# Starting a fused attention and MLP kernel with the v products of two x tiles, and spreading two chunks' row factors by a product

## The chip, the cores and the metric

The kernel runs on one core of one Trainium2 chip. Its engines are TensorE (PE, matrix products), VectorE (DVE), ScalarE (ACT), GpSimd (POOL) and SyncE (SP, which here issues nearly all DMAs); each works through its own queue of instructions in program order. The metric is the time of one execution in microseconds (us), as the median over several runs.

## The reference

The input x has 2048 rows of 512 numbers in bf16. The core of the reference, shortened:

```python
xn = layernorm(x)                       # no scale, no shift, eps 1e-5
q, k, v = split(xn @ wqkv)              # 32 heads of 16; row s attends to rows s, s-2, ..., s-14
s = softmax(q @ k_window * 0.25) @ v_window @ wo
h = gelu(layernorm(xn) @ w1)            # the norm is taken a second time
hs = shift_rows_by_group(h) @ w2        # four column groups, moved by +1, -1, +2, -2 rows
x1 = xn + hs
y = x1 + gelu(layernorm(x1) @ w3) @ w4  # w3: 512 x 1376, w4: 1376 x 512
out = x + s * silu(y)
```

The second norm acts on rows that are normed already, so it only multiplies each row by a factor close to 1, 1/sqrt(r² var + eps), where var is the variance of the row of x and r = 1/sqrt(var + eps). This text calls these the row factors.

## The kernel before

Rows are split by parity (even rows p = 0, odd rows p = 1), so that a window with a step of two becomes a plain window. Each half has two chunks of 512 rows, so there are chunks 0 to 3, and each chunk has four tiles of 128 rows. PSUM has eight banks: six are handed out as three pairs in turn (`pair`), two singly in turn (`single`, banks 6 and 7). Every instruction keeps its place in the program (`pin`), so the order of the calls in the text is the order on each engine's queue.

The first part of the kernel, up to about 50 us, is what the change touches. For each chunk it does this:

- `load_x` brings x tiles in. The loads stand first in SP's queue: four single tiles of chunk 0, then the q columns of wqkv, its v columns, its k columns (512 KB each), then chunk 1, w1 and chunk 2.
- `Norm.stats` (L217) takes mean and variance on DVE (`bn_stats`, `bn_aggr`); `root_act` (L223) gets 1/sqrt by ACT's Sqrt and a DVE reciprocal (chunk 0 only), `root` (L228) by two POOL instructions; `apply` (L231) norms in place on DVE.
- `turn` (L277) transposes two normed tiles by eight 128-wide products with the identity into one single bank, and DVE copies them to `xnT`.
- `rows2` (L244) computes the row factors r2, as 128 partitions x 4 numbers: for chunk 0 on DVE and ACT, for the others on POOL. `rows2_spread` (L260) must lay them along the free dimension, the same on all partitions: a PE transpose to 4 x 128, a DVE copy, a DMA to DRAM, and a DMA back that repeats the row over the 128 partitions into the last quarter of the tile `xn2T`. `scaled` (L269) multiplies `xnT` by it on DVE, and `w1` (L370) takes the product with w1 and a gelu on ACT.
- `q_half`, `q_all`, `k_all`, `v_mm`, `v_pair` are the projections; ACT moves their results out of PSUM: q as it is (`q_keep`), k twice with a mask `em` per head parity into `kM` (L327), v into a staging tile `vst` that must hold zeros elsewhere (L346), from where SP's queue writes it to DRAM (L350).

Before any data is there, twelve 128x512 products of ones (L139) run on PE, DVE clears `vst`, `zero` and the edges of `kM` and sums the identity into `em`. Chunk 0 is started by halves of 256 columns: two tiles are normed and transposed together, the q product of that half is taken, then v of two tiles, then the second half. Lines 488 to 549 are the order written out by hand. After them come w2 (L388), w3 and w4, and the attention in 18 blocks with the w4 products laid between.

Of the kernel before, what the change touches and what calls it, by code (L numbers as in the profile page):

```python
# [9 lines left out]
ALU = mybir.AluOpType  # L10
# [10 lines left out]
def kernel(  # L21
# [19 lines left out]
    def pin(ins):  # L41

        return tc.keep_in_program_order(ins)
# [38 lines left out]
    def b8(shape, name):  # L82
        return big.tile(shape, BF16, name=name, tag="b8")

    def b4(shape, name):
        return sm4.tile(shape, BF16, name=name, tag="b4")
# [4 lines left out]
    def pair():  # L91
        cnt["d"] += 1
        b = 2 * ((cnt["d"] - 1) % 3)
        return PS[:, b : b + 2, :]
# [8 lines left out]
    def load_x(c, t0, n):  # L103
        p, i = c // 2, (c % 2) * TPC + t0
        pin(SP.dma_start(
            out=xn[p][:, i : i + n, :], in_=xv[p, i * P : (i + n) * P, :].rearrange("(i q) d -> q i d", q=P)
        ))

    for t in range(TPC):
        load_x(0, t, 1)  # L110
    wqk_sb = b8([P, ND, 2 * D], "wqk_sb")
    pin(SP.dma_start(out=wqk_sb[:, :, 0:D], in_=wqkv_v[:, :, 0:D]))
    wv_sb = b4([P, ND, D], "wv_sb")
    pin(SP.dma_start(out=wv_sb, in_=wqkv_v[:, :, 2 * D : 3 * D]))
    pin(SP.dma_start(out=wqk_sb[:, :, D : 2 * D], in_=wqkv_v[:, :, D : 2 * D]))
    load_x(1, 0, 2)
    load_x(1, 2, 2)
# [17 lines left out]
    eps_t = const.tile([P, 1], F32, name="eps_t")  # L135
    pin(DVE.memset(eps_t[:], EPS))

    for i in range(12):
        pin(PE.matmul(  # L139
            PS[:, 6 + i % 2, :], lhsT=ones_bf[:], rhs=ones_bf.unsqueeze(1).to_broadcast([P, TPC, P]),  # L140
            start=True, stop=True,
        ))
# [12 lines left out]
    def head_masks():  # L155
        pin(DVE.tensor_reduce(
            out=em, in_=ident.rearrange("p (g e d) -> p e g d", e=2, d=16), op=ALU.add, axis=mybir.AxisListType.XY
        ))
# [49 lines left out]
    class Norm:  # L208
# [11 lines left out]
            for j in range(lo, hi):  # L220
                pin(DVE.bn_aggr(out=self.mv[:, j, :], in_=self.st[:, j, :]))

        def root_act(self, lo, hi):  # L223
            r = self.rstd[:, lo:hi]
            pin(ACT.activation(r, self.mv[:, lo:hi, 1], AF.Sqrt, bias=eps_t[:]))
            pin(DVE.reciprocal(out=r, in_=r))

        def root(self):  # L228
            rsqrt_eps(self.rstd, self.mv[:, :, 1])
# [8 lines left out]
    def x_of(c):  # L238
        p, k = c // 2, c % 2
        return xn[p][:, k * TPC : (k + 1) * TPC, :]  # L240
# [3 lines left out]
    def rows2(c, ln):  # L244

        r2 = small_t("r2", [P, TPC])
        r2b = small_t("r2b", [P, TPC], BF16)
        eng = DVE if c == 0 else POOL
        pin(eng.tensor_tensor(out=r2, in0=ln.rstd, in1=ln.rstd, op=ALU.mult))
        pin(eng.tensor_tensor(out=r2, in0=r2, in1=ln.mv[:, :, 1], op=ALU.mult))  # L250
        if c == 0:
            pin(ACT.activation(r2, r2, AF.Sqrt, bias=eps_t[:]))
            with nc.allow_low_precision("bf16 row factors"):
                pin(DVE.reciprocal(out=r2b, in_=r2))
        else:
            rsqrt_eps(r2, r2)
            pin(POOL.tensor_copy(out=r2b, in_=r2))
        r2s[c] = r2b

    def rows2_spread(c):  # L260
        pt = single().bitcast(BF16)[0:TPC, 0:P]
        pin(PE.transpose(pt, r2s[c], ident[:]))
        t = small_t("r2t", [TPC, P], BF16)
        pin(DVE.tensor_copy(out=t, in_=pt))
        pin(SP.dma_start(out=r2_d[c].rearrange("(j q) -> j q", q=P), in_=t))
        xn2Ts[c] = b4([P, ND, CH], "xn2T")
        pin(SP.dma_start(out=xn2Ts[c][:, ND - 1, :], in_=r2_d[c : c + 1, :].to_broadcast([P, CH])))

    def scaled(c):  # L269
        p, k = c // 2, c % 2  # L270
        t = xn2Ts[c]
        pin(DVE.tensor_tensor(
            out=t, in0=xnT[p][:, :, k * CH : (k + 1) * CH],
            in1=t[:, ND - 1, :].unsqueeze(1).to_broadcast([P, ND, CH]), op=ALU.mult,
        ))

    def turn(c, h):  # L277
        p, k = c // 2, c % 2
        i = k * TPC + 2 * h
        pt = single().bitcast(BF16).rearrange("p (a j q) -> p a j q", a=ND, j=2)  # L280
        for j in range(2):
            for dt in range(ND):
                pin(PE.transpose(pt[:, dt, j, :], xn[p][:, i + j, dt * P : (dt + 1) * P], ident[:]))  # L283
        pin(DVE.tensor_copy(
            out=xnT[p][:, :, i * P : (i + 2) * P], in_=pt.rearrange("p a j q -> p a (j q)")
        ))

    def q_half(pts, lo, hi):
        for nt in range(ND):
            for dt in range(ND):  # L290
                pin(PE.matmul(  # L291
                    pts[nt // 2][:, nt % 2, lo:hi], lhsT=wqk_sb[:, dt, nt * P : (nt + 1) * P],
                    rhs=xnT[0][:, dt, lo:hi], start=(dt == 0), stop=(dt == ND - 1),
                ))
# [21 lines left out]
            q_keep(c, a, proj(c, a, wqk_sb[:, :, 0:D], chunk(xnT, c)))  # L316

    def k_pad(p):
        pin(DVE.memset(kM[p][:, :, 0:8, :], 0.0))
        pin(DVE.memset(kM[p][:, :, M + 8 : MK, :], 0.0))  # L320

    def k_all(c):
        p, k = c // 2, c % 2
        for a in range(2):
            pt = proj(c, a, wqk_sb[:, :, D : 2 * D], chunk(xnT, c))
            for e in range(2):
                pin(ACT.activation(  # L327
                    kM[p][:, 2 * a : 2 * a + 2, 8 + k * CH : 8 + (k + 1) * CH, e], pt, AF.Copy, scale=em[:, e : e + 1]
                ))
# [3 lines left out]
    def v_mm(p, t, pt):  # L333
        for dt in range(ND):
            pin(PE.matmul(  # L335
                pt, lhsT=xnT[p][:, dt, t * P : (t + 1) * P], rhs=wv_sb[:, dt, :],
                start=(dt == 0), stop=(dt == ND - 1),
            ))

    def v_keep(p, t, n, pt, later=None):  # L340
        st = vst[vn["n"] % 2]
        vn["n"] += 1
        src = ap_of(pt, [pt.ap[0], [16, 2], [32, 16 * n], [1, 16]])
        d = st[:, 0, 0, :]
        dst = ap_of(d, [d.ap[0], [2 * D + 16, 2], [32, 16 * n], [1, 16]])
        pin(ACT.activation(dst, src, AF.Copy))  # L346

        def put():
            for i in range(n):
                pin(SP.dma_start(  # L350
                    out=v_d[p][8 + (t + i) * P : 8 + (t + i + 1) * P], in_=st[:, :, i, :]
                ))

        if later is None:
            put()
        else:
            later.append(put)

    def v_pair(p, t):
        pt = pair()  # L360
        for i in range(2):
            v_mm(p, t + i, pt[:, i, :])
        v_keep(p, t, 2, pt[:, 0, :])

    def v_pad(p):
        rows = v_d[p].rearrange("r e d -> (r e) d")
        pin(SP.dma_start(out=rows[0:16], in_=zero[0:16, :]))
        pin(SP.dma_start(out=rows[2 * (M + 8) : 2 * MK], in_=zero[0:4, :]))

    def w1(c, a):  # L370
        p, k = c // 2, c % 2
        pt = proj(c, a, w1_sb, xn2Ts[c])
        pin(ACT.activation(  # L373
            hT[p][:, 2 * a : 2 * a + 2, 1 + k * CH : 1 + (k + 1) * CH], pt, AF.Gelu_apprx_tanh
        ))
# [86 lines left out]
    for p in range(2):  # L462
        pin(POOL.memset(hT[p][:, :, 0:1], 0.0))
        pin(POOL.memset(hT[p][:, :, M + 1 : M + 2], 0.0))
        pin(POOL.memset(qT[p][:, :, M:MQ], 0.0))
    pin(DVE.memset(vst[0], 0.0))
    pin(DVE.memset(vst[1], 0.0))
    pin(DVE.memset(zero, 0.0))
    k_pad(0)
    k_pad(1)  # L470
    head_masks()
    l0 = Norm(x_of(0), x_of(0), TPC, "l1")
    l0.stats(0, 2)
    l0.root_act(0, 2)
    l0.apply(0, 2)
    l0.stats(2, 3)
    turn(0, 0)
    l0.stats(3, 4)
    l0.root_act(2, 4)
    l0.apply(2, 4)  # L480
    rows2(0, l0)
    pin(ACT.preload_act_table_set("gelu_apprx_tanh_and_others"))
    pq = [pair(), pair()]
    q_half(pq, 0, 2 * P)
    pv = pair()
    v_mm(0, 0, pv[:, 0, :])
    turn(0, 1)
    v_mm(0, 1, pv[:, 1, :])
    rows2_spread(0)
    v_keep(0, 0, 2, pv[:, 0, :])  # L490
    load_x(3, 0, 2)
    load_x(3, 2, 2)
    l1 = Norm(x_of(1), x_of(1), TPC, "l1")
    l1.stats(0, 4)
    l1.root()
    q_half(pq, 2 * P, CH)
    for a in range(2):
        q_keep(0, a, pq[a])
    cnt["d"] -= 1
    scaled(0)  # L500
    l1.apply(0, 4)
    rows2(1, l1)
    pin(SP.dma_start(out=w2_sb, in_=B_w2.rearrange("(g q) n -> q g n", q=P)))
    k_all(0)
    v_pair(0, 2)
    v_pad(0)
    l2 = Norm(x_of(2), x_of(2), TPC, "l1")
    l2.stats(0, 2)
    w1(0, 0)
    rows2_spread(1)  # L510
    pin(SP.dma_start(out=w3_sb, in_=B_w3.rearrange("(dt q) f -> q dt f", q=P)))
    turn(1, 0)
    turn(1, 1)
    w1(0, 1)
    l2.stats(2, 4)
    l2.root()
    l2.apply(0, 4)
    rows2(2, l2)
# [3 lines left out]
    scaled(1)  # L522
    q_all(1)
    k_all(1)
    rows2_spread(2)
    v_pair(0, 4)
    l3.apply(0, 4)
    rows2(3, l3)
    v_pair(0, 6)
    w1(1, 0)  # L530
    turn(2, 0)
    turn(2, 1)
    rows2_spread(3)
    w1(1, 1)
    scaled(2)
    q_all(2)
# [5 lines left out]
        in_=B_w4[0 : (NF - 1) * P, :].rearrange("(ft q) n -> q ft n", q=P),  # L542
    ))
    pin(SP.dma_start(out=w4_sb[0:FL, NF - 1, :], in_=B_w4[(NF - 1) * P : F, :]))
    w1(2, 0)
    w1(2, 1)
    scaled(3)
    w1(3, 0)
    w1(3, 1)
    w2(0)  # L550
# [401 lines left out]
```

## Time and profile before

The median of three runs is 201.47 us (201.37 to 202.03). The profiled execution took 201.1 us; its span, from the first to the last instruction, is 199.3 us.

| engine | busy us | share of the span |
|---|---|---|
| PE, products | 189.3 | 95% |
| PE, weight loads (beside the products) | 92.0 | 46% |
| ACT | 128.5 | 64% |
| DVE | 117.9 | 59% |
| POOL | 19.4 | 10% |

Busy time of PE includes the tail of each product, of which the next one covers most: a 128x512 product is listed with 379 ns, but in a dense run one starts every 216 ns, a 128x256 one every 109 ns and a 128x128 one every 56 ns. So starts are compared here, not ends. In the timeline a line gives start, length, engine, source line, operation, operands, count, and in brackets the idle time before it and what ended that. "L301" is line 301 of the kernel before; for a helper it is the same for all of its callers.

### The profile page before, as it was taken

Reading aid. Unit: us, or ns where it says so; the run is one execution under the profiler, and the core shown is the slowest. Engines: PE = TensorE matmul, PEld = TensorE weight load, DVE = VectorE, ACT = ScalarE, POOL = GpSimd, SP = SyncE. Lnnn points to the kernel's source line nnn. Section 1 sums busy time; section 2 is a strip of 40 time slices with the busy share of each in tenths; the row PEclk is TensorE's granted clock in tenths of the full one; section 3 lists DMA queues with packets and bytes.
Section 4 is the critical chain, followed back from the end, with each engine's and each line's share of the span. In section 5 each row is a group of like instructions: output and inputs, shape, how many; then the busy total and the mean of one; then the engine's idle time right before and its main releaser. Section 6 shows DMA issues by size and latency. Waiting matters only on the chain.

```text
span 199.3 us, 5290 instructions
## 1 busy us (share of the span) xinstructions
PE 189.3 (95%) x2285; PEld 92.0 (46%) x2285; DVE 117.9 (59%) x234; ACT 128.5 (64%) x143; POOL 19.4 (10%) x52
## 2 busy tenths in 40 slices
PE   7799999999999999999999999999999999999990
PEld 2464544554444444444444444554445445454540
DVE  7876785522076697585100034654769878796694
ACT  2188759558817615345564788687878868877850
POOL 1008058000002022015000000000000000000000
PEclk9999999999999999999999999999999999999997
DMA  5977655654000433853650062565944655762433
GB/s 129 369 239 240 216 119 209 221 174 135 0 0 3 132 83 105 210 107 106 149 170 0 0 187 79 166 193 151 268 134 122 166 167 150 175 188 71 146 105 105
DMA packets 33878, 28.37 MB, mean 142 GB/s; under 512 B 10808, under 2 KB 32832, under 8 KB 33856
## 3 DMA queue, kind: packets, MB, share of 16 engines
q1 hardware_dynamic: 33568, 27.84, 47.0%
q8 instruction: 18, 0.29, 0.6%
q10 hardware_dynamic: 288, 0.20, 0.3%
q14 instruction: 4, 0.03, 0.0%
HBM read 17.27 MB, written 8.67 MB: 130 GB/s over the span
## 4 chain that ended last, share of the span: by engine, by line
PE 79%; DVE 10%; ACT 4%; DMA 4%; issue 1%; SPq 0%; ACTq 0%; DVEq 0%
PE PS L442 19%; PE PS L301 17%; PE PS L729 16%; PE PS L776 7%; PE PS L400 4%; PE PS L335 4%; DMA ring<-rec_d 3%; ACT kM L327 3%; PE PS L617 3%; PE PS L591 2%; PE PS L760 2%; PE PS L291 2%; PE PS L627 2%; PE PS L283 1%; DVE l3s L219 1%; DVE xn L408 1%
## 5 line engine op out<-in xcount | busy, mean ns | idle before, releaser
L442 PE MATMUL PS<-x1nT,w_sb 128*128 128x512 bf16 (+1 forms) x176 | 38.3, 379 | 0.1
L598 ACT ACTIVATE prob<-PS 128x1824 bf16<-128x1824 f32 x18 | 30.4, 1688 | 5.4 <-PE PS L591 4.7
L729 PE MATMUL PS<-w_sb,h3a 128*128 128x512 bf16 x128 | 32.7, 380 | 0.7 <-DVE xn L742 0.7
L448 ACT ACTIVATE h3a<-PS 128x1024 bf16<-128x1024 f32 x16 | 16.4, 1023 | 20.9 <-PE PS L442 20.9
L742 DVE TENSOR_TENSOR xn<-PS,xn 128x512 bf16<-128x512 f32 x15 | 10.2, 680 | 30.7 <-PE PS L729 30.5
L442 PEld LDWEIGHTS <-w_sb 128*128 128x128 bf16 (+1 forms) x176 | 17.5, 100 | 20.8 <-DMA x1nT<-x1n_dram 0.6
L301 PE MATMUL PS<-xnT,wqk_sb 128*128 128x512 bf16 x112 | 25.0, 379 | 0.0
L327 ACT ACTIVATE kM<-PS,em 128x1024 bf16<-128x1024 f32 x16 | 20.6, 1401 | 3.7 <-PE PS L301 3.7
L603 DVE TENSOR_TENSOR prob<-prob,maskb 128x1824 bf16<-128x1824 bf16 x18 | 19.8, 1102 | 3.6 <-ACT prob L598 3.6
L408 DVE TENSOR_TENSOR xn<-PS,xn 128x1024 bf16<-128x1024 f32 x8 | 9.6, 1213 | 14.7 <-PE PS L400 14.7
L729 PEld LDWEIGHTS <-h3a 128*128 128x128 bf16 x128 | 11.3, 97 | 14.1 <-issue 1.9
L301 PEld LDWEIGHTS <-wqk_sb 128*128 128x128 bf16 x112 | 10.9, 98 | 12.7
L776 PE MATMUL PS<-wo_sb,oT 128*128 128x512 bf16 (+1 forms) x68 | 15.5, 366 | 0.0
L301 PE MATMUL PS<-xn2T,w_sb 128*128 128x512 bf16 x64 | 14.8, 379 | 0.1
L400 PE MATMUL PS<-w_sb,hT 128*128 128x512 bf16 x64 | 14.5, 379 | 0.1
L729 PE MATMUL PS<-w_sb,h3b 128*128 128x512 bf16 (+1 forms) x48 | 13.5, 381 | 0.0
L312 ACT ACTIVATE qT<-PS 128x1024 bf16<-128x1024 f32 x8 | 8.1, 1023 | 7.8 <-PE PS L301 7.7
L786 ACT ACTIVATE sg<-PS 128x512 bf16<-128x512 f32 x14 | 8.3, 596 | 6.2 <-PE PS L776 6.1
L346 ACT ACTIVATE vst<-PS 128x512 bf16<-128x512 f32 (+1 forms) x12 | 8.8, 744 | 3.5 <-ACT sig L749 2.4
L373 ACT ACTIVATE hT<-PS 128x1024 bf16<-128x1024 f32 x8 | 8.1, 1035 | 4.5 <-PE PS L301 4.5
L219 DVE BATCH_NORM_STATS2 l3s<-xn 128x6 f32<-128x512 bf16 x16 | 10.2, 682 | 0.2
L219 DVE BATCH_NORM_STATS2 l1s<-xn 128x6 f32<-128x512 bf16 x16 | 10.1, 677 | 0.0
(98 smaller groups left out, 225.7 us busy)
## 6 DMA issues: line engine op xcount, KB each, us to landing
ring<-v_d SPq DMA_DIRECT2D x18, 256.0 KB
v_d<-vst SPq DMA_DIRECT2D x16, 256.0 KB, 2.9
x1n_dram<-xn SPq DMA_DIRECT2D x4, 512.0 KB
xo<-in_A_x_dram SPq DMA_DIRECT2D x8, 256.0 KB, 4.0
ring<-rec_d SPq DMA_DIRECT2D x4, 456.0 KB, 5.2
out_dram<-xo SPq DMA_DIRECT2D x7, 256.0 KB, 3.1
xn<-in_A_x_dram SPq DMA_DIRECT2D x6, 256.0 KB, 4.1
w_sb<-in_B_w_dram SPq DMA_DIRECT2D x1, 1376.0 KB, 7.5
```

The costliest lines, as they stand in the source:

```text
L219: pin(DVE.bn_stats(out=self.st[:, j, :], in_=self.src[:, j, :]))
L301: pin(PE.matmul(pt[:, b, :], lhsT=w[:, dt, nt * P : (nt + 1) * P], rhs=rhs[:, dt, :], start=(dt == 0), stop=(dt == ND - 1),))
L327: pin(ACT.activation(kM[p][:, 2 * a : 2 * a + 2, 8 + k * CH : 8 + (k + 1) * CH, e], pt, AF.Copy, scale=em[:, e : e + 1]))
L400: pin(PE.matmul(pt[:, j, :], lhsT=w2_src(p, g, m0), rhs=w2_sb[:, g, :], start=(g == 0), stop=(g == ND - 1),))
L408: pin(DVE.tensor_tensor(out=xs, in0=pts[h], in1=xs, op=ALU.add))
L442: pin(PE.matmul(pt[:fs, ft % 2, :], lhsT=w3_sb[:, dt, ft * P : ft * P + fs], rhs=x1nT[:, dt, :], start=(dt == 0), stop=(dt == ND - 1),))
L448: pin(ACT.activation(t[:, o : o + 2, :], pt, AF.Gelu_apprx_tanh))
L598: pin(ACT.activation(pr, S_ps[:, :, 0 : ND * NQ], AF.Exp, scale=SCALE))
L603: pin(DVE.tensor_tensor(out=f, in0=f, in1=maskb[:], op=ALU.min))
L729: pin(PE.matmul(pt, lhsT=h3_of(c, ft)[:fs, jj * P : (jj + 1) * P], rhs=w4_sb[:fs, ft, :], start=(ft == 0), stop=(ft == NF - 1 and silu < 2),))
L742: pin(DVE.tensor_tensor(out=x_i, in0=pt, in1=x_i, op=ALU.add))
L776: pin(PE.matmul(pt[:, 0:W], lhsT=oT[p][:, dt, i * P : (i + 1) * P], rhs=wo["sb"][:, dt, c], start=(dt == 0), stop=(dt == ND - 1),))
```

## The change

- Loads: after two x tiles the v columns come, then the other two x tiles, then the q columns. The issuing queue is the same.
- Ten products of ones instead of twelve.
- Filling with zeros moves: one `vst` tile to ACT (a Copy with scale 0 of 128x2048), `zero` and the edges of `kM` to POOL, one `vst` tile stays on DVE. The sum for `em` moves behind the second transpose copy.
- The first two x tiles are normed one by one (`root_act` is split into its ACT and its DVE half). Each is transposed by `turn_one` into a single bank of its own, and ACT copies it.
- The v products of these two tiles come first on PE, then a quarter of q at a time with the transposes of the other two tiles between.
- `rows2_here` replaces `rows2_spread` for chunks 0 and 3: DVE multiplies the identity by the row factors into 128x512 diagonal blocks, one product with ones puts the sums, which are the factors, on every partition, and ACT (chunk 0) or DVE (chunk 3) copies them to `xn2T`. No DRAM is used for these two.
- The k product of chunk 0 is split around `v_pair(0, 2)`; the statistics of chunks 1 and 2 move, and `rows2_spread(2)` moves behind two `v_pair` calls, whose stores then stand before its two DMAs in SP's queue.

```diff
@@ -106,12 +106,14 @@
 
-    for t in range(TPC):
-        load_x(0, t, 1)
     wqk_sb = b8([P, ND, 2 * D], "wqk_sb")
+    wv_sb = b4([P, ND, D], "wv_sb")
+    load_x(0, 0, 1)
+    load_x(0, 1, 1)
+    pin(SP.dma_start(out=wv_sb, in_=wqkv_v[:, :, 2 * D : 3 * D]))
+    load_x(0, 2, 1)
+    load_x(0, 3, 1)
     pin(SP.dma_start(out=wqk_sb[:, :, 0:D], in_=wqkv_v[:, :, 0:D]))
-    wv_sb = b4([P, ND, D], "wv_sb")
-    pin(SP.dma_start(out=wv_sb, in_=wqkv_v[:, :, 2 * D : 3 * D]))
     pin(SP.dma_start(out=wqk_sb[:, :, D : 2 * D], in_=wqkv_v[:, :, D : 2 * D]))
@@ -135,7 +137,7 @@
 
-    for i in range(12):
+    for i in range(10):
         pin(PE.matmul(
@@ -220,10 +222,12 @@
 
-        def root_act(self, lo, hi):
+        def root_act(self, lo, hi, half=None):
             r = self.rstd[:, lo:hi]
-            pin(ACT.activation(r, self.mv[:, lo:hi, 1], AF.Sqrt, bias=eps_t[:]))
-            pin(DVE.reciprocal(out=r, in_=r))
+            if half != 1:
+                pin(ACT.activation(r, self.mv[:, lo:hi, 1], AF.Sqrt, bias=eps_t[:]))
+            if half != 0:
+                pin(DVE.reciprocal(out=r, in_=r))
 
@@ -266,6 +270,21 @@
 
+    def rows2_here(c):
+        xn2Ts[c] = t = b4([P, ND, CH], "xn2T")
+        d = t[:, 0, :].rearrange("p (j q) -> p j q", q=P)
+        pin(DVE.tensor_tensor(
+            out=d, in0=ident.unsqueeze(1).to_broadcast([P, TPC, P]), in1=r2s[c].unsqueeze(2).to_broadcast([P, TPC, P]),
+            op=ALU.mult,
+        ))
+        pt = single()
+        pin(PE.matmul(pt, lhsT=ones_bf[:], rhs=t[:, 0, :], start=True, stop=True))
+        if c == 0:
+            pin(ACT.activation(t[:, ND - 1, :], pt, AF.Copy))
+        else:
+            pin(DVE.tensor_copy(out=t[:, ND - 1, :], in_=pt))
     def scaled(c):
@@ -285,8 +304,16 @@
 
-    def q_half(pts, lo, hi):
-        for nt in range(ND):
+    def turn_one(c, t):
+        p, k = c // 2, c % 2
+        i = k * TPC + t
+        pt = single().bitcast(BF16)[:, 0 : ND * P].rearrange("p (a q) -> p a q", a=ND)
+        for dt in range(ND):
+            pin(PE.transpose(pt[:, dt, :], xn[p][:, i, dt * P : (dt + 1) * P], ident[:]))
+        pin(ACT.activation(xnT[p][:, :, i * P : (i + 1) * P], pt, AF.Copy))
+    def q_half(pts, lo, hi, nts=range(ND)):
+        for nt in nts:
             for dt in range(ND):
@@ -316,12 +343,12 @@
     def k_pad(p):
-        pin(DVE.memset(kM[p][:, :, 0:8, :], 0.0))
-        pin(DVE.memset(kM[p][:, :, M + 8 : MK, :], 0.0))
-
-    def k_all(c):
+        pin(POOL.memset(kM[p][:, :, 0:8, :], 0.0))
+        pin(POOL.memset(kM[p][:, :, M + 8 : MK, :], 0.0))
+    def k_all(c, parts=(0, 1)):
         p, k = c // 2, c % 2
-        for a in range(2):
+        for a in parts:
             pt = proj(c, a, wqk_sb[:, :, D : 2 * D], chunk(xnT, c))
@@ -463,56 +490,64 @@
         pin(POOL.memset(qT[p][:, :, M:MQ], 0.0))
-    pin(DVE.memset(vst[0], 0.0))
-    pin(DVE.memset(vst[1], 0.0))
-    pin(DVE.memset(zero, 0.0))
+    pin(POOL.memset(zero, 0.0))
     k_pad(0)
     k_pad(1)
-    head_masks()
+    pin(ACT.activation(
+        vst[0].rearrange("p e i d -> p (e i d)").rearrange("p (a q) -> p a q", q=P),
+        ones_bf.unsqueeze(1).to_broadcast([P, 16, P]), AF.Copy, scale=0.0,
+    ))
+    pin(DVE.memset(vst[1], 0.0))
     l0 = Norm(x_of(0), x_of(0), TPC, "l1")
-    l0.stats(0, 2)
-    l0.root_act(0, 2)
-    l0.apply(0, 2)
-    l0.stats(2, 3)
-    turn(0, 0)
-    l0.stats(3, 4)
+    for t in range(2):
+        l0.stats(t, t + 1)
+        l0.root_act(t, t + 1, 0)
+    for t in range(2):
+        l0.root_act(t, t + 1, 1)
+        l0.apply(t, t + 1)
+    turn_one(0, 0)
+    turn_one(0, 1)
+    pv = pair()
+    for t in range(2):
+        v_mm(0, t, pv[:, t, :])
+    l0.stats(2, 4)
     l0.root_act(2, 4)
...
     rows2(0, l0)
+    v_keep(0, 0, 2, pv[:, 0, :])
     pin(ACT.preload_act_table_set("gelu_apprx_tanh_and_others"))
     pq = [pair(), pair()]
-    q_half(pq, 0, 2 * P)
-    pv = pair()
-    v_mm(0, 0, pv[:, 0, :])
+    q_half(pq, 0, 2 * P, (0, 1))
     turn(0, 1)
-    v_mm(0, 1, pv[:, 1, :])
-    rows2_spread(0)
-    v_keep(0, 0, 2, pv[:, 0, :])
+    q_half(pq, 0, 2 * P, (2, 3))
+    head_masks()
     load_x(3, 0, 2)
     load_x(3, 2, 2)
-    l1 = Norm(x_of(1), x_of(1), TPC, "l1")
-    l1.stats(0, 4)
-    l1.root()
-    q_half(pq, 2 * P, CH)
+    q_half(pq, 2 * P, CH, (0, 1))
+    rows2_here(0)
+    q_half(pq, 2 * P, CH, (2, 3))
     for a in range(2):
         q_keep(0, a, pq[a])
-    cnt["d"] -= 1
+    l1 = Norm(x_of(1), x_of(1), TPC, "l1")
+    l1.stats(0, 2)
     scaled(0)
+    l1.stats(2, 4)
+    l1.root()
     l1.apply(0, 4)
...
     pin(SP.dma_start(out=w2_sb, in_=B_w2.rearrange("(g q) n -> q g n", q=P)))
-    k_all(0)
+    k_all(0, (0,))
     v_pair(0, 2)
+    k_all(0, (1,))
     v_pad(0)
-    l2 = Norm(x_of(2), x_of(2), TPC, "l1")
-    l2.stats(0, 2)
     w1(0, 0)
...
     w1(0, 1)
-    l2.stats(2, 4)
+    l2 = Norm(x_of(2), x_of(2), TPC, "l1")
+    l2.stats(0, 4)
     l2.root()
@@ -522,15 +557,14 @@
     k_all(1)
-    rows2_spread(2)
     v_pair(0, 4)
...
     v_pair(0, 6)
+    rows2_spread(2)
     w1(1, 0)
...
     turn(2, 1)
-    rows2_spread(3)
     w1(1, 1)
@@ -542,9 +576,10 @@
     pin(SP.dma_start(out=w4_sb[0:FL, NF - 1, :], in_=B_w4[(NF - 1) * P : F, :]))
+    rows2_here(3)
+    scaled(3)
     w1(2, 0)
     w1(2, 1)
-    scaled(3)
     w1(3, 0)
```

## The prediction

> **What bounds the kernel now.** First the page's busy times and its 40 slices:
>
> ```profile
> PE 189.3 (95%) x2285; PEld 92.0 (46%) x2285; DVE 117.9 (59%) x234; ACT 128.5 (64%) x143; POOL 19.4 (10%) x52
> ...
> PE   7799999999999999999999999999999999999990
> ```
>
> PE is the bound from the third slice on; only the first two have room. A gain must come from starting the real products sooner, or from one of the few later holes. So next PE's timeline of the start, and who PE waited for:
>
> ```profile
> 1.12 4.75 PE L139 MATMUL PS<-ones_bf 128*128 128x512 bf16 x12 [1.12 <-DVE ones_bf L132]
> 6.25 0.72 PE L283 MATMUL PS<-ident,xn 128*128 128x128 bf16 x8 [0.38 <-DVE xn L233]
> 7.96 1.91 PE L291 MATMUL PS<-xnT,wqk_sb 128*128 128x256 bf16 x16 [0.99 <-DVE xnT L284]
> ...
> 11.97 0.22 PE L262 MATMUL PS<-ident,r2b 128*4 128x128 bf16 x1
> 12.12 1.92 PE L291 MATMUL PS<-xnT,wqk_sb 128*128 128x256 bf16 x16
> 13.88 3.62 PE L301 MATMUL PS<-xnT,wqk_sb 128*128 128x512 bf16 x16
> ```
>
> The first projection starts at 7.96, the k product of chunk 0 at 13.88, and nothing waits between. After that the only hole before 50 us is here:
>
> ```profile
> 36.00 1.06 PE L283 MATMUL PS<-ident,xn 128*128 128x128 bf16 x16
> 37.40 0.22 PE L262 MATMUL PS<-ident,r2b 128*4 128x128 bf16 x1 [0.34 <-DVE xnT L284]
> 37.54 1.90 PE L301 MATMUL PS<-xn2T,w_sb 128*128 128x512 bf16 x8
> ```
>
> The row factors of chunk 3 take a single bank that DVE is still emptying. What led to 7.96 is on DVE:
>
> ```profile
> 1.24 0.91 DVE L466 MEMSET vst<- 128x1024 uint32 x1 [0.16 <-issue]
> 2.32 0.91 DVE L467 MEMSET vst<- 128x1024 uint32 x1 [0.16 <-issue]
> ...
> 3.72 1.28 DVE L219 BATCH_NORM_STATS2 l1s<-xn 128x6 f32<-128x512 bf16 x2
> 4.92 0.30 DVE L221 BATCH_NORM_AGGREGATE l1m<-l1s 128x2 f32<-128x6 f32 x2
> 5.58 0.17 DVE L226 RECIPROCAL l1r<-l1r 128x2 f32<-128x2 f32 x1 [0.36 <-ACT l1r L225]
> 5.78 0.73 DVE L233 TENSOR_SCALAR xn<-xn,l1m,l1r 128x512 bf16<-128x512 bf16 x2
> ```
>
> DVE clears buffers until 3.7, although the trace's landing records have x tile 0 there at 3.02 and tile 1 at 3.44. Last, the loads, as bytes moved in 40 slices of the first 16 us (0.4 us each):
>
> ```profile
> GB/s 0 0 0 0 38 248 236 251 241 297 102 49 305 325 379 364 364 394 379 382 394 376 374 364 379 384 389 358 361 346 346 348 315 87 5 0 0 61 90 197
> ```
>
> The x tiles move from 1.8 to 4.0, then there is a dip, and from 4.8 the big loads stream at about 370 GB/s. They land in the order of issue: x2 4.02, x3 4.52, q columns 6.97, v 8.42, k 9.66.
>
> **The change part by part.** All from the one profiled execution: 201.1 us, span 199.3. The median of the runs, 201.47, is 0.37 above it.
>
> *Loads.* A 512 KB load begins moving some 2.1 us after its issue (q columns: issued at 2.67, stream from 4.75), and lands about 0.75 after its last byte (6.17 by 524 KB at 370 GB/s, seen 6.97). The v columns will be issued third, at 1.73: moving from 3.8, landed near 6.0. x2 and x3 follow in the stream, 0.35 each: 6.3 and 6.6. The q columns, 1.42 more: 8.1. Bounds for the v columns: 4.9 (x1's 3.44 plus the 1.45 between the q and v landings) and 6.97 (where the first big load lands now). I take 6.0, since it follows from the issue times.
>
> *DVE and ACT before the norm.* DVE keeps one fill of 0.91 and is free at 2.15. ACT's fill comes after its table load (0.80 + 1.28): 128x512 from SBUF takes 0.635 (the tanh row), the slope between the 128x512 and 128x1824 evictions (0.596 and 1.688) is 0.83 ns an element, so 1.9 us, to 4.0. POOL's fills have no reader before the v stores; they cost nothing.
>
> *Norm and transposes singly.* Statistics of tile 0 from 3.05, 0.68; aggregate to 3.93; Sqrt (0.30) to 4.3, just behind ACT's fill. Statistics of tile 1 from 3.9, aggregate to 4.76, Sqrt to 5.1. DVE: reciprocal and apply of tile 0 (0.17, 0.41) to 5.33, of tile 1 to 5.9. Transposes (four, 0.39 with their tail) from 5.39, the tenth product of ones having streamed out by then: the records start 0.427 apart up to the tenth, at 4.94. The two products that are left out would have stood in front of them (the last now starts at 5.50). ACT's copies: no row shows 128x512 bf16 from PSUM; between 0.55 (128x456) and 1.02 (128x1024) I take the f32 128x512, 0.60. They end at 6.4 and 7.0. The v products: 6.46 to 8.19 (eight by 0.216), v columns there since 6.0.
>
> *The quarters of q.* Columns at 8.1 cost nothing; at 8.42, where the second big load lands now, 0.25. I take 0.1. Eight by 0.109: to 9.1. Tiles 2 and 3: statistics from 6.4, aggregate 7.95, Sqrt 8.3, reciprocal 8.5, applied 9.25. Their transposes end at 9.6; next quarter to 10.5. The DVE copy is queued behind `rows2`, whose reciprocal waits for ACT's Sqrt (two products of 0.16, Sqrt 0.30, reciprocal 0.18): free at 10.16, copy 0.69, so PE waits from 10.5 to 10.9. Quarter to 11.8; behind the copy DVE does `em` (0.27) and the diagonal, a 128x512 product, 0.43 by the row of that shape, 0.67 at the slow end: ready at 11.5 to 11.8. Product 0.22, last quarter 0.87: the k product starts at 12.9 instead of 13.88. **Gain at the start 1.0.**
>
> *Banks after that.* v staged on ACT 9.95 to 10.97, table load 1.28, copy of the factors 0.60, q 2 x 1.02 to 14.9, four k copies 1.29 apart and the v copy between to 21.1. Each pair is free before PE needs it, the tightest the first w1 product (17.5 against 18.05). In exchange the round trip through DRAM is gone: `scaled(0)` moves from 16.99 to about 13.3, off the path either way.
>
> *Row factors of chunk 1.* DVE statistics end near 15.9; POOL's chain takes 3.6 as chunk 2's does (24.48 to 28.07): 19.6, against PE's need at 19.8. With the 4.6 it takes now (15.19 to 19.8, where one POOL step took 1.12 beside `scaled(0)`) PE would wait 0.8. The new order keeps `scaled(0)` ahead of that chain, so I take 3.6 and nothing.
>
> *Chunk 3 by a product.* The transpose goes from 37.40, so w1 starts right behind the turns: the last transpose starts at 36.84, takes 0.06, and w1 comes at 36.90 instead of 37.54. **Gain 0.64.** The new product (0.22) stands before `w1(2,0)`; there PE waits 0.22 two steps later, at 50.5, for ACT's k copies (from 45.55, 5.16 long), so it is paid from that wait: nothing. Uncovered it would cost 0.22.
>
> *rows2_spread(2).* Now its DMAs are issued behind four v stores: those end at 37.65 now, so about 36.5 then; write 1.7, read 3.2: landed at 41.5. DVE: `scaled(2)` 1.2, two copies 1.3, diagonal 0.6: 44.6, while PE reaches the new product at 45.4. Margin 0.8; with the slowest of the four reads (4.0) it is just gone. From the transpose's move itself PE gains or loses nothing.
>
> Sum: 201.1 - 1.0 - 0.64 = 199.45; from the median, 199.8. Every later hole (67.8, 71.5, the reciprocal round trips) begins with a PE product, so the shift is carried to the end.
>
> **The rivals.**
>
> *Everything in the first stream is late.* The v columns land at 6.97, the q columns at 9.1. v ends at 8.7, q starts at 9.1, tiles 2 and 3 are applied at 10.2, and k starts at 13.8: the start brings 0.1, in all 0.75: 200.7. For it: no load of that size has landed sooner. Against: it is issued 0.94 sooner.
>
> *The stream is early.* v columns at 4.9: tiles 2 and 3 in time, no wait behind `rows2`; q at 7.0. k starts at 12.2: 1.7 + 0.64, so 199.1.
>
> *Chunk 3's gain does not come.* The new product waits for the diagonal because `scaled(2)` waits for its DMA in DVE's queue; a read landing 1.5 later than worked out takes the 0.64 back: 200.45.
>
> *PE's clock, slower than before.* The first nine products of ones start 0.427 apart, the last two 0.217: the clock doubled at about 5.19, after 4.07 us of unbroken work, while the page's clock row shows full speed there. Now the real products can wait for this, as only transposes stand before 7.96. Afterwards they begin at 5.39 and have small holes. If the doubling came only at T, PE would lose half of what it works between 5.39 and T; with 85% busy, 1.65 is lost at T = 9.3, and at T = 12 the loss is 2.8: 202.6. For: two products fewer; against: ten at the slow pitch cover 1.12 to 5.39. The Trainium skill (TensorE: Matmul & The Clock Gate, "What's actually happening") has the gate watch free-running windows of about 3.4 us, whose phase differs from run to run; by that rule the doubling could come anywhere from 4.5 to 7.9 us here, which would cost, as an estimate from that page, up to about 0.7 in some runs and leave 199.8 to 200.5, and the one trace agrees with it at 5.19 without telling the phase of other runs.
>
> **How the numbers follow.** Forecast 0.46, own range 199.3 to 200.3; early stream 0.14; late stream 0.16; chunk 3 lost 0.12; clock or another wait of over 1.65, 0.12. A measurement of this kernel can tell about 0.3% (0.6 us) from no change. Faster takes the first four less the part of the late cases that add up: 0.78; same 0.10; slower 0.12. The range leaves out half of the early case (below 199.0) and the slower one: 199.0 to 201.1.
>
> **What would show it.** v products starting near 6.5 and k of chunk 0 near 12.9; a PE wait of about 0.4 for the second transpose copy; w1 of chunk 1 without a hole; no wait before the new product near 45. Wrong: PE waiting for a load before the v or q products, products of 512 columns starting 0.427 apart after 5.4, or DVE reaching the diagonal of chunk 3 after PE.

## The result, and the profile after

The changed kernel took 199.5 us as a median of four runs (198.76 to 199.72), the kernel before 201.42; the ratio is 0.9893 with a 95% interval of 0.9859 to 0.9928. Measured once more beside the experiments it took 199.95 against 201.71, ratio 0.9911 [0.9879, 0.9942]. The forecast was 199.8, the range 199.0 to 201.1. Every ratio here is to the kernel before as timed beside the kernel in question (medians 201.11 to 201.71), over the fast runs alone, which are those within 1.5% of a kernel's fastest; only for e2 does that leave any out. The profiled execution is the fastest of the first four: 198.76 us, span 197.0.

From the page of the changed kernel, busy times and the 40 slices:

```profile
PE 185.4 (94%) x2253; PEld 91.7 (47%) x2283; DVE 117.6 (60%) x229; ACT 132.3 (67%) x148; POOL 19.1 (10%) x57
...
PE   7899999999999999999999999999999999899990
```

PE is as dense as before, and still the bound; ACT has 3.8 us more to do. (The count of PE's products is of records, some of which are missing in this trace.) The timeline of PE at the start:

```profile
1.12 4.03 PE L141 MATMUL PS<-ones_bf 128*128 128x512 bf16 x10 [1.12 <-DVE ones_bf L134]
5.51 0.91 PE L312 MATMUL PS<-ident,xn 128*128 128x128 bf16 x8 [0.37 <-DVE xn L237]
6.60 1.90 PE L362 MATMUL PS<-wv_sb,xnT 128*128 128x512 bf16 x8 [0.17 <-ACT xnT L313]
8.49 1.05 PE L318 MATMUL PS<-xnT,wqk_sb 128*128 128x256 bf16 x8
9.37 0.61 PE L302 MATMUL PS<-ident,xn 128*128 128x128 bf16 x8
9.82 2.08 PE L318 MATMUL PS<-xnT,wqk_sb 128*128 128x256 bf16 x16
11.73 0.38 PE L282 MATMUL PS<-xn2T,ones_bf 128*128 128x512 bf16 x1
11.95 1.04 PE L318 MATMUL PS<-xnT,wqk_sb 128*128 128x256 bf16 x8
12.82 1.89 PE L328 MATMUL PS<-xnT,wqk_sb 128*128 128x512 bf16 x7
```

The first line that counts is the third: real products start at 6.60, not 7.96. The last shows what it is worth: the k product of chunk 0 starts at 12.82 instead of 13.88, 1.06 us sooner. The second hole, in the same timeline:

```profile
34.94 1.06 PE L302 MATMUL PS<-ident,xn 128*128 128x128 bf16 x16
35.84 1.89 PE L328 MATMUL PS<-xn2T,w_sb 128*128 128x512 bf16 x8
...
45.36 0.38 PE L282 MATMUL PS<-xn2T,ones_bf 128*128 128x512 bf16 x1
45.58 4.73 PE L328 MATMUL PS<-xn2T,w_sb 128*128 128x512 bf16 x20
```

The w1 product follows the transposes with no transpose of row factors between, and the new product at 45.36 has no wait in front of it. To follow a shift through the kernel, starts of ACT's instructions serve best, as each waits for a PE product. Differences to the kernel before, first profiles:

| instruction of ACT | before | after | difference |
|---|---|---|---|
| first k copy, chunk 1 | 29.04 | 27.98 | -1.06 |
| first k copy, chunk 2 | 45.56 | 43.84 | -1.72 |
| first gelu behind w3 | 73.95 | 72.27 | -1.68 |
| first exp | 115.62 | 113.93 | -1.69 |
| last exp | 181.43 | 179.24 | -2.19 |

So 1.06 comes from the start, 0.66 from chunk 3, and in this pair of profiles both are carried through the next 70 us. The last 0.5 arose in the attention part, at two waits for DMAs (before blocks 9 and 14). A second pair (e7 for the kernel before, e8 for the changed kernel) has -1.05, -1.71, -1.46, -1.46 and, at the last exp, +0.11: the gain of the first 50 us is the same, and the attention part of that one execution, the slowest of six, took all of it back. How much of it arrives on average only the medians tell.

### The profile page after: what moved, and what is told of

The parts are those of the page before. It is cut to its first block, busy times and chain, and to the rows that moved or that the text cites. A ratio compares the mean times of both kernels' runs of the same rounds, so it can differ in the third digit from the quotient of the medians.

```text
span 197.0 us, 5251 instructions
## 1 busy us (share of the span) xinstructions
PE 185.4 (94%) x2253; PEld 91.7 (47%) x2283; DVE 117.6 (60%) x229; ACT 132.3 (67%) x148; POOL 19.1 (10%) x57
## 4 chain that ended last, share of the span: by engine, by line
PE 85%; DVE 7%; DMA 3%; issue 2%; ACT 2%; DVEq 0%; ACTq 0%
PE PS L469 19%; PE PS L328 19%; PE PS L764 18%; PE PS L811 6%; PE PS L427 4%; PE PS L362 4%; PE PS L795 3%; PE PS L652 3%; PE PS L626 3%; PE PS L318 2%; DMA ring<-v_d 2%; PE PS L302 2%; PE PS L662 2%; DVE l3s L221 1%; DVE xn L435 1%
## 5 line engine op out<-in xcount | busy, mean ns | idle before, releaser
L764 PE MATMUL PS<-w_sb,h3a 128*128 128x512 bf16 x112 | 29.2, 379 | 2.5 <-issue 1.8
L764 PE MATMUL PS<-w_sb,h3b 128*128 128x512 bf16 (+1 forms) x44 | 12.8, 380 | 0.8 <-issue 0.8
```

The source lines that it names most:

```text
L764: pin(PE.matmul(pt, lhsT=h3_of(c, ft)[:fs, jj * P : (jj + 1) * P], rhs=w4_sb[:fs, ft, :], start=(ft == 0), stop=(ft == NF - 1 and silu < 2),))
```

## The experiments

Two theories stood against each other: that of the prediction (two independent gains, 1.0 and 0.64, carried to the end), and that one part does it all, or that a part is only needed to make room for another. Unless a text says otherwise, each kernel computes the whole result.

### Chunk 3 through DRAM again (e1, and again as e12)

```diff
     turn(2, 1)
+    rows2_spread(3)
     w1(1, 1)
...
-    rows2_here(3)
-    scaled(3)
     w1(2, 0)
     w1(2, 1)
+    scaled(3)
```

> The changed kernel, only with the row factors of chunk 3 sent through DRAM again (transpose behind the turns of chunk 2). My theory: the hole before the first w1 product of chunk 1's second half comes back, so all that follows is 0.64 us later than in the changed kernel; the 0.22 us of the removed product show up as a longer wait for ACT's k copies at about 48.4. Time 200.1. Rival (the hole was covered by something later, and the whole gain is from the start): no difference, 199.5.

Measured: 200.08 us, 0.9962 [0.9933, 0.9991] of the kernel before. PE's timeline in e1 has the old hole, of the same 0.34 us:

```profile
34.95 1.06 PE L302 MATMUL PS<-ident,xn 128*128 128x128 bf16 x16
36.34 0.22 PE L266 MATMUL PS<-ident,r2b 128*4 128x128 bf16 x1 [0.34 <-DVE xnT L303]
36.49 1.90 PE L328 MATMUL PS<-xn2T,w_sb 128*128 128x512 bf16 x8
```

From the first k copy of chunk 1 to that of chunk 2 pass 16.51 us, in the changed kernel 15.85; in the two profiles of the kernel before 16.51 both times, in the other kernels with the product 15.85 or 15.86 without exception. That is 0.66, free of all else. The new product's 0.22 shows up where the theory put it: from the first w1 product of the second half (46.03) to the first w2 product (53.16) pass 7.13 us in e1, in the changed kernel 6.94 (45.58 to 52.52), so the removed product came back as 0.19 of waiting.

> The changed kernel with the row factors of chunk 3 through DRAM, as in e1, beside e11 on one chip. My theory: 16.51 us again in place of 15.85, and 1.0 us of the gain left: ratio 0.994 to 0.9965. Rival (chunk 3 brings nothing to the time, as e4 says): ratio 0.991, as for the changed kernel itself.

Measured: 200.28 us, 0.9958 [0.9936, 0.9980], and 16.51 us again. The time agrees with the theory.

### The kernel before, with chunk 3 by the product alone (e4, and again as e11)

The helper `rows2_here` is added as it stands in the changed kernel; the calls change so:

```diff
-    rows2_spread(3)
     w1(1, 1)
...
+    rows2_here(3)
+    scaled(3)
     w1(2, 0)
     w1(2, 1)
-    scaled(3)
```

> The kernel before, only with the row factors of chunk 3 spread by the product. My theory: the hole at 37.4 us goes, everything behind is 0.64 us earlier, and the new product is covered by the wait for ACT's k copies at 50.5; time 200.8. Rival (the product is on the path): 0.42 us, 201.0; rival (no effect): 201.4.

Measured: 201.06 us, 0.9999 [0.9980, 1.0018]. The trace has 15.85 us, so the gain is there, but not in the time. In e4 PE waited 0.20 longer in the transposes at 21.4, and here:

```profile
64.13 7.31 PE L415 MATMUL PS<-w_sb,hT 128*128 128x512 bf16 x31
71.85 4.48 PE L457 MATMUL PS<-x1nT,w_sb 128*128 128x512 bf16 x20 [0.41 <-DMA x1nT<-x1n_dram]
```

This wait for the transposing DMA stands between the last w2 product before it and the first w3 product. From start to start that is 0.79 us in e4; in the first profile of before it is 0.52, where the DMA landed at 71.97 and DVE's l3m ended at 71.98, just ahead of the w3 product at 72.01. So e4 lost up to 0.27 more here.

> The kernel before with the row factors of chunk 3 by the product, as in e4, for another profile and more times. In e4's profile the hole was gone (15.85 us instead of 16.51 between the first k copy of chunk 1 and that of chunk 2), but the time did not move. My theory: the 0.65 are there again and are partly lost at later waits for DMAs, which differ from one execution to the next; 0.2 to 0.5 remain in the time, ratio 0.9975 to 0.999. Rival (a DMA that does not move along with PE takes it all back): ratio 1.000, and the same later wait is longer by 0.4 or more in both profiles.

Measured: 200.97 us, 0.9980 [0.9957, 1.0002]. This profile has 15.85 us too, and the distance at 71 is 0.55: the first exp comes at 115.00, 0.62 before the first profile of before. So the longer wait for x1nT belongs to the execution, not to the kernel (the distance is 0.56 in the second profile of before, 0.53 and 0.82 in the two of the changed kernel).

The rival's DMA is in the attention part. DVE's reciprocals of a block (`rec`) go to DRAM and come back into `ring`, and DVE, and PE behind it, waits for them before block 9. In the chain that ended last, the kernel before has:

```profile
135.57 2.33 DMA rec_d<-rec
...
137.92 5.25 DMA ring<-rec_d
```

The second write is issued 19.95 or 19.96 us behind the first exp in all fourteen profiles, so it does move along with PE, and the rival as worded falls. But the trip, from this issue to the landing, took 7.14 to 8.34 us, and the distance from exp 8 to exp 9 follows it: 3.87 at 7.14, 3.99 at 7.40 (the changed kernel's first profile), 4.19 at 7.60 (above), 4.58 at 7.99 (e11), 4.94 at 8.34. In e4 and e11 the trip took 7.87 and 7.99, in the two profiles of before 7.60 and 7.36. Two profiles of each can't tell whether that is chance. Whether the whole 0.66 reaches the time was not resolved: by their ratios the two kernels gain 0.0 and 0.4 us, and the two with the part undone (e1, e12) lose 0.9 to 1.0 against 0.9911.

### The old load order (e2)

```diff
     load_x(0, 1, 1)
-    pin(SP.dma_start(out=wv_sb, in_=wqkv_v[:, :, 2 * D : 3 * D]))
     load_x(0, 2, 1)
     load_x(0, 3, 1)
     pin(SP.dma_start(out=wqk_sb[:, :, 0:D], in_=wqkv_v[:, :, 0:D]))
+    pin(SP.dma_start(out=wv_sb, in_=wqkv_v[:, :, 2 * D : 3 * D]))
```

> The changed kernel with the loads in the order of the kernel before: x tiles 0 to 3, q columns, v columns. My theory: the v columns land at 8.4 us as before, the v products start there instead of at 6.6, tiles 2 and 3 are normed sooner (about 8.3), so the k product of chunk 0 starts near 14.3 instead of 12.8: 1.5 us lost, more than the start brought; time 201.0. Rival (the loads arrive in time in any order, the start is set by the norm): below 0.3 us.

Measured: 1.0033 [0.9985, 1.0080] of the kernel before, over 200.24, 202.05 and 203.20 us; the other seven of the ten runs took 203.31 to 205.37, and the profile is of one of these, 204.17. PE's timeline in it:

```profile
5.51 1.13 PE L312 MATMUL PS<-ident,xn 128*128 128x128 bf16 x8
9.73 3.31 PE L362 MATMUL PS<-wv_sb,xnT 128*128 128x512 bf16 x8 [3.08 <-DMA wv_sb<-in_A_wqkv_dram]
12.84 1.33 PE L318 MATMUL PS<-xnT,wqk_sb 128*128 128x256 bf16 x8
```

PE stood for 3.08 us before the v products, and these took 3.1 us to issue instead of 1.73. The same execution by stretches (start:end, length, busy us and count of PE, weight loads, DVE, ACT, POOL, then the granted clock, DMA share, GB/s):

```profile
0.00:6.60 6.60, 5.48 (x18) 2.03 (x18) 4.42 (x14) 4.18 (x5) 1.65 (x17) 1.00 0.61 183
6.60:10.00 3.40, 0.32 (x3) 0.25 (x3) 2.10 (x9) 1.27 (x4) 0.00 (x0) 1.00 1.08 383
10.00:13.40 3.40, 3.40 (x11) 1.35 (x10) 0.00 (x0) 0.26 (x1) 0.00 (x0) 0.50 1.02 332
13.40:20.00 6.60, 6.55 (x52) 4.62 (x52) 5.34 (x12) 5.19 (x6) 0.00 (x0) 1.00 0.69 188
```

(The 1.00 of the first row stands ahead of the first clock record, at 6.61, and is not to be trusted: the products of ones start 0.427 apart there.) PE was nearly idle for 3.4 us, and the clock was 0.50 for the next 3.4. In this execution the k product of chunk 0 starts at 17.36, where the theory had 14.3: 1.3 because the v columns landed at 9.68 instead of 8.4, and some 1.7 because the work behind them ran at half clock (7.63 us from the first v product to the k product, while the same products at their dense spacing make 5.9). The fall of the clock is likely in most executions, as the mean granted clock over the run says: 0.980 to 0.989 in nine of the ten runs and 0.998 in the one of 200.24 us, while the runs of all other kernels lie at 0.991 or above, but for e5's (0.987 to 0.996), whose clock doubled late. So the load order is not one gain among others: without it nothing of the gain is left (1.0033 against 0.9911 for the changed kernel). Whether v first with the old loads is slower than the kernel before, the ratio leaves open. The theory had the sign and the place and missed the clock.

### Chunk 0 through DRAM again (e3)

```diff
     q_half(pq, 0, 2 * P, (2, 3))
+    rows2_spread(0)
     head_masks()
...
-    rows2_here(0)
...
-    l1.stats(0, 2)
-    scaled(0)
-    l1.stats(2, 4)
+    l1.stats(0, 4)
     l1.root()
+    scaled(0)
     l1.apply(0, 4)
```

> The changed kernel with the row factors of chunk 0 sent through DRAM again, with the multiplication by them behind the statistics of chunk 1 as in the kernel before. My prediction called this part off the path either way: the multiplication should end near 18.2, when PE needs it at 18.0, so at most 0.2 us lost, and the time 199.5 to 199.7. Rival: the shift of the start can't be had without the product, since the DMAs (issued behind the v stores) come after 18; then PE waits before the first w1 product, by as much as 1.0 to 1.5 us, and the time is 200.5 to 201.0.

Measured: 201.94 us, 1.0048 [1.0017, 1.0078]: slower than the kernel before. PE's timeline in e3 has two new waits:

```profile
9.99 1.05 PE L318 MATMUL PS<-xnT,wqk_sb 128*128 128x256 bf16 x8 [1.41 <-DMA wqk_sb<-in_A_wqkv_dram]
...
17.65 1.89 PE L328 MATMUL PS<-xnT,wqk_sb 128*128 128x512 bf16 x8
20.23 1.89 PE L328 MATMUL PS<-xn2T,w_sb 128*128 128x512 bf16 x8 [0.69 <-DMA xn<-in_A_x_dram]
```

The first is the q columns, landed at 9.95 in this execution; the edit's first DMA is issued at 12.78, so this is not its doing. The second is the rival's. The releaser named there had long been done; DVE's timeline shows whom PE waited for, and SP's why:

```profile
18.85 1.23 DVE L291 TENSOR_TENSOR xn2T<-xnT,xn2T 128x2048 bf16<-128x2048 bf16 x1 [3.25 <-DMA xn2T<-r_d]
```

```profile
10.88 1.30 SPq L377 DMA_DIRECT2D v_d<-vst  x2
12.78 0.34 SPq L269 DMA_DIRECT2D r_d<-r2t  x1
15.44 0.37 SPq L271 DMA_DIRECT2D xn2T<-r_d  x1
```

The write of the factors and its receipt took 2.7 us (12.78 to 15.44), behind the v stores, the read another 3.4; the multiplication ended at 20.08, when the k products had long streamed out (17.65 + 8 x 0.216 = 19.38). That is 0.85 lost here, although PE itself was late by the first wait. Had the q columns come at 8.44 as in the first profile, the k products would have ended at 17.9, while the two DMAs could not start before the v stores are issued at 12.2; with the same lengths w1 would start at 19.6, an estimate of 1.75 lost from these rows. Both waits together put the first k copy of chunk 1 at 30.20, 2.22 behind the changed kernel. The median, 201.94, is 2.0 to 2.4 above the changed kernel's and beyond what either theory forecast; how much of that is a late load in the other nine executions, no profile shows. So the product for chunk 0 is what lets the shift of the start get past the first w1 product.

### Six products of ones (e5)

```diff
-    for i in range(10):
+    for i in range(6):
```

> The changed kernel with six products of ones instead of ten, so PE idles from about 3.7 to 5.5 us. This tells what the clock rival would cost. If the doubling of the clock hangs on unbroken work ahead of it, it comes later than the 5.2 us seen, the v products start 0.427 apart, and the start loses 0.5 to 1.7 us: 200.0 to 201.2. Rival (the clock doubles at a fixed time, or as soon): no difference, 199.5.

Measured: 201.25 us, 1.0000 [0.9976, 1.0024]: in the time the whole gain is gone. PE's timeline in e5:

```profile
1.12 2.74 PE L141 MATMUL PS<-ones_bf 128*128 128x512 bf16 x6 [1.12 <-DVE ones_bf L134]
5.44 1.13 PE L312 MATMUL PS<-ident,xn 128*128 128x128 bf16 x8 [1.58 <-DVE xn L237]
6.74 2.94 PE L362 MATMUL PS<-wv_sb,xnT 128*128 128x512 bf16 x8 [0.17 <-ACT xnT L313]
9.51 1.04 PE L318 MATMUL PS<-xnT,wqk_sb 128*128 128x256 bf16 x8
```

The v products are spread over 2.77 us instead of 1.89, up to the q product; the clock records have the doubling at 8.87. The first k copy of chunk 0 comes at 15.66 instead of 14.75, 0.91 later. So the doubling depends on the work ahead of it, and the rival's fixed instant falls. The trace shows 0.91 lost at the start and chunk 3's gain still there (15.85); the rest of the loss lies in the attention part of this execution (66.64 us from the first exp to the last, 65.31 in the changed kernel's first profile), which differs between executions.

### All fills on DVE (e6, and again as e10)

The zeros of both `vst` tiles, of `zero` and of the edges of `kM`, and the sum for the masks, stand on DVE ahead of the statistics again; nothing else differs from the changed kernel.

```diff
-    pin(POOL.memset(zero, 0.0))
+    pin(DVE.memset(vst[0], 0.0))
+    pin(DVE.memset(vst[1], 0.0))
+    pin(DVE.memset(zero, 0.0))
     k_pad(0)
     k_pad(1)
-    pin(ACT.activation(
...
-    pin(DVE.memset(vst[1], 0.0))
+    head_masks()
...
-    head_masks()
```

(In `k_pad` the engine changes from POOL to DVE.)

> The changed kernel with all fills on DVE again, ahead of the statistics, and the sum for the masks there too. My theory: the statistics of tile 0 start at 3.7 instead of 3.25, the v products at about 7.05, and since the q columns hold PE at 8.44 anyway, 0.3 us are lost: 199.8. Rival (the q columns set the start): none lost, 199.5.

Measured: 201.16 us, 1.0007 [0.9979, 1.0035]. In DVE's timeline of e6 the first statistics start where they did before, 0.47 later than in the changed kernel (3.25):

```profile
3.72 0.68 DVE L221 BATCH_NORM_STATS2 l1s<-xn 128x6 f32<-128x512 bf16 x1
```

The v products start at 7.06, the first k copy of chunk 1 is 0.25 later than in the changed kernel. The place is as forecast, the time missed the forecast by 1.4.

> The changed kernel with all fills on DVE ahead of the statistics, as in e6, now beside the changed kernel on one chip. By its trace it lost 0.25 us at the start, by its time 1.7. If the rest was the chip or chance, it is 0.25 to 0.5 above the changed kernel here; if the fills cost something that the first 60 us of the trace do not show, it is 1 us or more above.

Measured: 200.89 us, 0.9969 [0.9946, 0.9992], beside 199.95 for the changed kernel. The trace shows 0.34 (first k copy of chunk 1 at 28.40 against 28.06), the medians 0.9. Both measurements agree that the fills cost more in time than at the start of the trace. At the first exp the two profiles are still only 0.31 and 0.10 behind, and their attention parts (66.58 and 66.37 us) lie within the changed kernel's own two (65.31 and 66.98). Where the rest is lost stays open.

### The kernel before (e7) and the changed kernel (e8) again

> The kernel before, unchanged, for a second profile. The profile of the changed kernel is 2.3 us faster, of which 1.7 arise before 60 us, and 0.5 in the attention part, at two waits near 144 and 160 us. If these 0.5 are chance of one execution, this profile has these two waits of another length than the first (0.38 us each); if they follow from the change, they are the same, 0.38 each, in both profiles of the kernel before.

Measured: 200.83 us, one execution. From the first exp to the last pass 65.42 us, in the first profile 65.81; the spacings of exps 8 to 9 and 13 to 14 are 3.95 and 4.09, before 4.19 and 4.24. In the changed kernel's first profile they are 3.99 and 3.95.

> The changed kernel, unchanged, for more profiles and times beside the next two on one chip. So far the q columns (512 KB) landed at 8.44, 8.55, 8.78, 9.09 and 9.95 in five profiles of kernels with the new load order, and the first quarter of q started with them, while in the kernel before nothing waited for them. My theory: what the change gains varies with this landing, 1.7 us where it is 8.4 and less by what it is later; here 199.5 to 200.3. Rival (the four runs so far show it all): 199.5.

Measured: 199.95 us; its profiled execution took 200.75 and has 4.73 and 4.86 at these two spacings, 66.98 in all. So the two waits vary by up to 0.9 each between executions of one kernel, and the 0.5 of the first profile is well within that: chance. This profile's start, in PE's timeline:

```profile
8.66 1.05 PE L318 MATMUL PS<-xnT,wqk_sb 128*128 128x256 bf16 x8 [0.24 <-DMA wqk_sb<-in_A_wqkv_dram]
```

The q columns landed at 8.62. Over all profiles with the new order and one q load it was 8.44, 8.45, 8.55, 8.62, 8.78, 9.09 and 9.95 (and 8.91 as the start of q in e12). The start does follow this landing where it is late: the first k copy of chunk 0 comes at 14.75 in the first profile, at 15.07 in e12 and at 16.12 in e3. The median lies in the forecast range, but the theory does not explain the spread of these six runs, 198.96 to 200.75: the slowest is the profiled one, and its q columns cost 0.07 at the first k copy (14.82), its attention part 1.67.

### The q columns in two loads (e9)

```diff
-    pin(SP.dma_start(out=wqk_sb[:, :, 0:D], in_=wqkv_v[:, :, 0:D]))
+    for h in range(0, D, 2 * P):
+        pin(SP.dma_start(out=wqk_sb[:, :, h : h + 2 * P], in_=wqkv_v[:, :, h : h + 2 * P]))
```

> The changed kernel with the q columns loaded by two DMAs of 256 columns each, since the first quarter of q needs only the first half of them. My theory: the first half lands some 0.7 us sooner, the quarter starts right behind the v products (8.33), and the k product of chunk 0 comes 0.15 us sooner than in the first profile of the changed kernel, by 0.7 in executions with late loads; time 0.2 to 0.6 below that of the changed kernel beside it. Rival (rows of 512 bytes slow the stream, or an issue more delays it): the k columns land later, no gain or 0.3 lost.

Measured: 199.87 us, 0.9910 [0.9882, 0.9938], beside 199.95 and 0.9911. In the trace it does what it should:

```profile
6.73 1.90 PE L363 MATMUL PS<-wv_sb,xnT 128*128 128x512 bf16 x8 [0.17 <-ACT xnT L314]
8.46 1.04 PE L319 MATMUL PS<-xnT,wqk_sb 128*128 128x256 bf16 x8
```

Eight v products at 0.216 end at 8.46, and q follows at once, its half having landed at 7.49. The first k copy comes at 14.62 instead of 14.75 and 14.82. The forecast of 0.2 to 0.6 in the time was missed; a gain of 0.1 to 0.2 is below what the times can tell, and none is shown.

Not undone one at a time were the norm by single tiles, ACT's copies of the transposes and the v products' place ahead of q, nor was the new load order run in the kernel before. Their shares of the 1.06 are therefore known only from the timeline.

## Why the prediction was right

- **Loads.** The v columns were put at 6.0, x2 at 6.3, x3 at 6.6, the q columns at 8.1; they landed at 6.28, 6.59, 6.97 and 8.44. The scheme (fixed delay behind the issue, then one stream in order) holds; of the 0.3, a little is arithmetic, as the rows it was read from give 0.80 behind the last byte (6.17 to 6.97), not 0.75, and two steps of 0.35 from 6.0 end at 6.7. What failed is the treatment of the q columns as a term of 0.1 with bounds of 0 and 0.25: PE waited 0.16 for them in the first profile, and 1.41 in the worst, and a wait for a load before the q products was on the prediction's own list of signs of being wrong. The rival "everything in the first stream is late" had the right load, but took the v columns for the cause; in the profiles the v columns are steady (5.85 to 6.28) and the q columns are not.
- **Norm, transposes, v products.** Statistics at 3.25 instead of 3.05 (x tile 0 landed at 3.23), v products at 6.60 instead of 6.46. ACT's copies took 0.597, as the f32 row has it, ACT's fill 1.91 against 1.9.
- **The quarters of q.** The wait for the second transpose copy was priced at 0.4; the starts show it as 0.17 (the quarter ends at 10.69, the next starts at 10.86), because PE came 0.16 later with the q columns. Two errors that nearly cancel, which is luck: the k product was forecast for 12.9 and came at 12.82.
- **scaled(0) "off the path either way".** This sentence was wrong, as e3 shows. It was written of the changed kernel, where the multiplication is early, but claimed for the DMA way too, and it gave the product for chunk 0 no share of the gain. Without it PE waits for w1.
- **Row factors of chunk 1.** POOL's chain ran from 15.62 to 19.24, 3.6 as taken, and PE did not wait at 19.82.
- **Chunk 3.** Forecast 0.64, shown 0.66. The new product was expected at 45.4 and came at 45.36. The margin of DVE was put at 0.8 and was 0.2, so this came closer to failing than forecast: the multiplication by chunk 2's factors, expected from 41.5, started at 42.12 behind its DMA, and chunk 3's diagonal ended at 45.13, as DVE's timeline has it:

```profile
42.12 1.23 DVE L291 TENSOR_TENSOR xn2T<-xnT,xn2T 128x2048 bf16<-128x2048 bf16 x1 [5.24 <-DMA xn2T<-r_d]
43.26 1.28 DVE L303 COPY xnT<-PS 128x1024 bf16<-128x1024 bf16 x2
44.45 0.68 DVE L277 TENSOR_TENSOR xn2T<-ident,r2b 128x512 bf16<-128x512 bf16 x1
```

- **Carried to the end.** The sum was 1.64; the first exp shows 1.69 in one pair of profiles and 1.46 in the other. The attention part adds or takes more than 1 us per execution (65.31 and 66.98 us for the changed kernel), which the prediction did not count. The medians give 1.8 to 1.9, so on average the gain arrives; the 0.3 by which the first four runs came under the forecast is within the spread of the runs.
- **The clock.** The rival for the other side had a real mechanism: e5 and e2 show it with its price. It did not come in any of the eight profiles with ten products of ones and the new load order: the clock doubled at 6.56 at the latest, and the v products started behind it each time, though in e9 (6.54 and 6.73) only by 0.19. So ten products were enough in these executions; a later doubling in others is not ruled out.

## What to carry to other kernels

A load order and an order of work can be one edit: here the order of work kept nothing of the gain without its load order (e2), and nothing without the product for chunk 0 (e3). What a replaced transfer was worth is seen only when the work in front of it becomes sooner. A load that is moved behind others has a landing that varies from execution to execution; if nothing stands between it and its reader, price the spread, not one landing. And where waits for DMAs move by a microsecond between runs, a distance between two instructions that belong to the edit (here 16.51 against 15.85) settles what the times can't.

## What was not expected of the hardware

The instant at which PE's clock doubles, from the trace's clock records, was 3.80, 3.97, 4.58, 4.84, 5.98, 6.37, 6.54, 6.56 and 6.61 us in nine profiles of kernels with the same ten products of ones, and 5.19, 5.29, 5.59 and 6.65 with twelve. In e2 it doubled at 6.61, fell at 10.03 and doubled at 13.44: steps of 3.41 each. With six products it did not double before 8.87. The Trainium skill (TensorE: Matmul & The Clock Gate, "What's actually happening") says of such windows that they run free of the kernel's start; these instants agree. It asks for a busy window; in the profile with 3.80 PE had worked for 2.7 of the 3.41 us ahead of it, which was enough, while in e5 the 1.8 us of work in the window that ended one step ahead of 8.87 were not. So the doubling can come earlier than the 4.5 us that the prediction worked out for a whole window of work.
